# One block's decays and one of its key/query turns by DMA in place of TensorE, with the steps around them placed anew, in a fused linear-attention and bilinear-FFN kernel

## Chip, cores and metric

The kernel runs on 1 core of one Trainium2 chip. The metric is device microseconds from launch to end, less is better. Engines in the profile: PE is TensorE's matmul, PEld its weight load, DVE is VectorE, ACT is ScalarE, POOL is GpSimd, SP is SyncE, which here only issues DMAs.

## What is computed

The reference is a gated linear attention followed by a bilinear feed-forward layer:

```python
batch, n_heads, seq, head_dim = (4, 8, 768, 48)      # q, k, v, alpha
for t in range(S):
    state = alpha[:, :, t, :, None] * state + np.einsum('bhd,bhe->bhde', k[:, :, t], v[:, :, t])
    y[:, :, t] = np.einsum('bhd,bhde->bhe', q[:, :, t], state)
...
n_tokens, d_model, d_ff = (3072, 384, 1536)
x = np.ascontiguousarray(attn_out.transpose(0, 2, 1, 3)).reshape(B * S, H * D)
a = x @ w_a
b = x @ w_b
return (a * b @ w_out).astype(np.float32)
```

Inputs and output are float32; alpha lies between 0.8 and 1.0.

## The kernel before

The work is cut into six blocks, called chunks in the code and numbered 0 to 5. Block c holds the positions of third `c // 2` of the sequence (256 of 768) for two of the four batches; its two batches are its rows 0 and 1. Blocks 0 and 1 are the first third of the sequence, and the state goes from block 0 to 2 to 4 and from 1 to 3 to 5. Two neighbouring positions share a partition (`r`), and the 128 partitions are two halves (`g`) of 64, between which the state is carried on.

The whole order of work is written out by hand in the string `PROGRAM` (from L17). A line names a block and a list of steps; the table `OPS` maps each step's first word to a function, its arguments are a row, a half, a PSUM bank (0 to 7) or an engine (V = DVE, S = ACT, P = GpSimd, Y = SP). Each engine takes its own steps in the order in which they stand there, and waits where a step needs another engine's result, a bank that is still being read, or a buffer that is still in use. A step on one engine never overtakes an earlier one on the same engine. So the place of a step in `PROGRAM` matters only against other steps of its own engine or DMA queue.

The steps of a block, with those that the change and the prediction touch:

- `ld` loads q, k, v or alpha, from the queue of GpSimd or SP (L547). `Wo` loads the output weights. `ln`, `l2`, `l2s`, `ra` make logarithms of alpha, their pair sums `l2`, and `ra` (L554, L562, L611, L643).
- `H`, `L` split `l2` into a rounded part and a rest (L599, L605); `A2 u bank` sums them over the positions on PE (L636). In later blocks `R` and `AQ` do this (L621, L631).
- `E u b` and `E u i` take exponentials of that sum on ACT: `beta` and `invb` (L665). `lv` scales q by `ra` and k by alpha (L650). `mq`, `mk` write the scaled queries and keys into `QKp` (L676, on DVE).
- The decays of the state, one number for each batch, half, head and feature, go into the small tile `bl`. Two ways exist. `dk` makes them on PE with two-column matmuls (`decay_pe`, L698) and `de` takes the exponential on ACT (`decay_exp`, L719). Or `dr` stores the last row of each half of `beta` to a DRAM tile `row` (L682) and `dl` loads it back feature by feature into `bl` (L687); both are SP's DMAs, two for each step.
- Queries and keys have to be turned, features onto partitions. Two ways exist here too. `C u h bank` turns half a row's heads with eight PE transposes (`turn`, L736) and `Ce u h engine` copies the 1024 columns from PSUM into `kqT` (L958 on ACT or L960 on DVE). Or `T u` turns the whole row with one DMA transpose from SP (`turn_dma`, L745), and `Tr u engine` sorts the keys into another tile, `kp` (`turn_keys`).
- `K2` multiplies keys and values on PE (L805) into two banks, one for each half; `k u g` folds them into the state, using `bl` (`state`: L819, or L822 and L823; on DVE). The first half gives `Sm`, the second `S`.
- `D u h bank` makes scores on PE in two banks (L837), `Mc` with `Mm`, or `M`, masks them. `SB` and `SA` multiply the queries by the carried state and `Y` the scores by the values, both L866; `v`, `vs` prepare the values; `X` copies the result to `xT`.
- The feed-forward: `a f w bank` and `b f w bank` are three matmuls each (L921) for one of twelve groups f of 128 of the 1536 columns, 512 columns wide for both rows (`*`) or 256 for one row. `as` copies a's result from PSUM on ACT (L927), `pr` multiplies it by b's on DVE (L935), `o m half bank` is six matmuls for half the sum of output tile m (L943), `ot` copies it out and `st` stores it.

Until the change, blocks 0 and 1 use PE for decays and turns, and blocks 2 to 5 use DMA:

```python
def decay_rows(ch, us):
    for g in range(2):
        nc.sync.dma_start(out=ch.row[us, g:g + 1].rearrange("b g a r d -> g b (a r d)"),
                          in_=ch.beta[(g + 1) * HC - 1:(g + 1) * HC, us].rearrange("g b h d -> g b (h d)"))

def decay_load(ch, us):
    for r in range(2):
        nc.sync.dma_start(out=bls[ch.c % 2][r * DP:r * DP + D, us].rearrange("d b g a -> d (b g a)"),
                          in_=ch.row[us, :, :, r, :].rearrange("b g a d -> d (b g a)"), allow_slow_non_contiguous=True)

def turn_dma(ch, u):
    nc.sync.dma_start_transpose(out=alloc_t(ch, u).rearrange("p (x s) -> p x s", s=C), in_=QKp[ch.c % 2][:, u].rearrange("p j r h d -> p (j r h d)"))
```

Of the kernel before, what the change touches and what calls it, by code (L numbers as in the profile page):

```python
# [102 lines left out]
2: AQ 0; E 1 i; ld v * P; E 1 b  # L103
1: pr 2 0; a 10 0 4; as 10 0; a 7 0 5; M 1 0; a 1 0 6; Mm 1 1 V; b 4 0 7; pr 4 0; b 1 0 1; a 5 0 4; as 1 0
1: pr 1 0
2: lv 0 q P; E 0 b; dr
1: b 10 0 6; pr 10 0; a 6 0 7; as 7 0; b 7 0 1; pr 7 0; b 5 0 5; as 5 0
2: lv 1 k P
1: b 11 0 6; pr 5 0; SA 1
2: mq 0 V  # L110
1: Y 1
2: mq 1 V
1: b 6 0 1
2: mk 1 V; E 0 i
1: as 6 0; a 0 0 0; b 0 0 7; pr 6 0; a 11 0 4; X 1 S; a 2 1 5; b 3 0 2; as 0 0; pr 0 0; as 11 0; a 3 0 3
1: as 3 0; a 8 0 4; b 9 0 0; b 2 1 1; a 6 1 3; pr 11 0; as 2 1; a 9 0 5; as 9 0; pr 3 0; o 2 0 2
3: ln *; l2s 0 P; l2 0 P
0: st 0 Y
1: a 5 1 5; pr 2 1
# [1058 lines left out]
```

## Time and profile before

| | |
|---|---|
| median of 3 runs | 189.72 us |
| lowest and highest | 189.21 and 191.22 us |
| the profiled execution's own time | 190.44 us |
| its span, first to last instruction | 188.7 us |
| mean granted TensorE clock | 0.991 |
| DMA, whole execution | 29.43 MB, mean 156 GB/s |
| DMA queues of SP | 41.2% of 16 engines' span |
| DMA queue of GpSimd | 39.3% of 16 engines' span |

The profile shows one execution. Times in it count from the first instruction. In a group's row stand the line, the engine, the operation, the tiles (written <- read), the shapes and the count; then busy time, mean length, and the idle time before with what ended it. In a timeline a row has start, length, engine, line, operation and tiles, and in brackets the engine's idle time before it with its releaser. The chain of waits follows the work that ended last back to the start, so its shares add up to the span. Matmuls are pipelined: the step from one group's start to the next tells a group's price better than its length.

### The profile page before, as it was taken

The numbers are of one execution on the slowest core, as the hardware profiler recorded it, in microseconds if no ns is written. First come the engines' busy times: TensorE is split into PE (matmuls) and PEld (weight loads), VectorE is DVE, ScalarE is ACT, GpSimd is POOL, SyncE is SP. The second block draws the span as 40 slices with busy tenths as digits, with TensorE's granted clock in tenths as the row PEclk, the third lists the DMA queues.
The fourth block names the chain that finished last, engine by engine and source line by source line (L and its number), as shares of the span: only waits on it lengthen the run. The fifth ranks groups of instructions, "written<-read, shape, count | busy, mean of one in ns | idle before, by whom it ended". The sixth has DMA issues, their size and how long they took to land.

```text
span 188.7 us, 6347 instructions
## 1 busy us (share of the span) xinstructions
PE 181.9 (96%) x2693; PEld 122.3 (65%) x2709; DVE 152.6 (81%) x271; ACT 120.1 (64%) x228; POOL 53.6 (28%) x74
## 2 busy tenths in 40 slices
PE   7979999999999999999999999999999999999993
PEld 3969886566778886754445644555457477565992
DVE  2484889788979799998889899999999945696862
ACT  4364865579995797797697949965980451526230
POOL 8999654998062240003500003300000000000000
PEclk9987999999999999999999999999999999999999
DMA  5999999999999899989999699939500102110053
GB/s 125 263 225 195 261 235 254 230 231 257 247 214 129 129 215 276 275 237 182 198 173 271 144 116 167 112 107 165 89 0 9 43 0 83 44 43 0 0 170 127
DMA packets 66285, 29.43 MB, mean 156 GB/s; under 512 B 55776, under 2 KB 64624, under 8 KB 66256
## 3 DMA queue, kind: packets, MB, share of 16 engines
q1 hardware_dynamic: 47488, 16.34, 41.2%
q0 software_dynamic: 18624, 12.58, 39.3%
q8 instruction: 21, 0.34, 0.7%
q10 hardware_dynamic: 144, 0.10, 0.2%
q14 instruction: 8, 0.07, 0.1%
HBM read 25.98 MB, written 4.74 MB: 163 GB/s over the span
## 4 chain that ended last, share of the span: by engine, by line
PE 90%; ACT 6%; issue 2%; DVE 1%
PE psum L921 47%; PE psum L943 12%; PE psum L1032 11%; PE psum L866 5%; PE psum L837 3%; PE psum L589 2%; PE psum L590 2%; PE psum L736 2%; PE psum L572 2%; ACT vx L958 2%; PE psum L631 1%; ACT la L554 1%; PE psum L792 1%; PE psum L805 1%; PE psum L698 1%
## 5 line engine op out<-in xcount | busy, mean ns | idle before, releaser
L921 PE MATMUL psum<-xT,wb_t 128*128 128x512 bf16 (+1 forms) x263 | 55.8, 336 | 0.5 <-issue 0.2
L921 PE MATMUL psum<-xT,wa_t 128*128 128x512 bf16 (+1 forms) x262 | 55.2, 335 | 0.5 <-issue 0.2
L921 PEld LDWEIGHTS <-wa_t 128*128 128x128 bf16 x270 | 25.7, 98 | 19.2 <-issue 0.5
L921 PEld LDWEIGHTS <-wb_t 128*128 128x128 bf16 x270 | 25.5, 98 | 18.4 <-issue 0.5
L943 PE MATMUL psum<-wo_t,prod 128*128 128x384 bf16 x144 | 26.1, 327 | 0.0
L958 ACT ACTIVATE ot<-psum 128x384 f32<-128x384 f32 (+1 forms) x23 | 11.2, 487 | 17.7 <-PE psum L1032 15.4
L650 POOL TENSOR_TENSOR q_t<-q_t,ra 128x384 f32<-128x384 f32 x6 | 6.4, 1072 | 53.6 <-ACT ra L643 31.1
L943 PEld LDWEIGHTS <-prod 128*128 128x128 bf16 x144 | 13.3, 98 | 8.3
L958 ACT ACTIVATE vx<-v_t 32x384 bf16<-32x384 bf16 x26 | 13.5, 521 | 1.5 <-DVE vx L771 1.1
L1032 PEld LDWEIGHTS <-prod 128*128 128x128 bf16 x144 | 12.0, 98 | 1.2
L850 ACT ACTIVATE m<-psum 128x768 bf16<-128x768 f32 x14 | 11.0, 810 | 2.3 <-PE psum L837 2.3
L676 DVE TENSOR_TENSOR QKp<-q_t,beta 128x768 bf16<-128x768 f32 x10 | 9.4, 952 | 1.9 <-ACT beta L665 1.6
L554 ACT ACTIVATE la<-a_t 128x1536 f32<-128x1536 f32 (+2 forms) x9 | 9.5, 1054 | 1.7 <-DMA a_t<-in_alpha_dram 1.5
L676 DVE TENSOR_TENSOR QKp<-k_t,invb 128x768 bf16<-128x768 f32 x10 | 10.1, 1013 | 0.3
L846 DVE TENSOR_TENSOR m<-psum,mask 128x768 bf16<-128x768 f32 x10 | 9.5, 949 | 0.6 <-PE psum L837 0.6
L1044 DVE TENSOR_TENSOR ot<-psum,ot 128x384 f32<-128x384 f32 x9 | 5.0, 555 | 5.9 <-issue 3.2
L866 PE MATMUL psum<-m,vx 64*64 64x128 bf16 (+1 forms) x576 | 8.7, 205 | 0.0
L547 POOL DMA_DIRECT2D v_t<-in_v_dram x8 | 8.5, 1064 | 0.0
L866 PE MATMUL psum<-kqT,Sm 64*64 64x128 bf16 x144 | 7.5, 220 | 0.4 <-DVE Sm L819 0.4
L866 PEld LDWEIGHTS <-vx 64*64 64x64 bf16 x576 | 7.6, 108 | 0.1
L854 DVE TENSOR_TENSOR m<-m,mask 128x768 bf16<-128x768 bf16 x14 | 7.4, 550 | 0.0
L665 ACT ACTIVATE prod<-psum 128x384 f32<-128x384 f32 x8 | 3.5, 488 | 6.0 <-PE psum L590 6.0
(292 smaller groups left out, 361.5 us busy)
## 6 DMA issues: line engine op xcount, KB each, us to landing
out_dram<-ot SPq DMA_DIRECT2D x23, 192.0 KB, 2.7
q_t<-in_q_dram SPq DMA_DIRECT2D x3, 768.0 KB
k_t<-in_k_dram SPq DMA_DIRECT2D x3, 768.0 KB
a_t<-in_alpha_dram POOLq DMA_DIRECT2D x2, 768.0 KB, 11.7
v_t<-in_v_dram POOLq DMA_DIRECT2D x4, 384.0 KB, 7.6
a_t<-in_alpha_dram SPq DMA_DIRECT2D x2, 768.0 KB
a_t<-in_alpha_dram POOLq DMA_DIRECT2D x3, 384.0 KB, 7.5
k_t<-in_k_dram POOLq DMA_DIRECT2D x3, 384.0 KB, 7.3
```

What stands on the lines that cost most here:

```text
L547: eng.dma_start(out=t[:, us, hs].rearrange("p b h r d -> p (b h) (r d)"), in_=src[ch.b0 + us.start:ch.b0 + us.stop, hs, ch.s * 2 * C:(ch.s ...
L554: nc.scalar.activation(out=ch.la[:, us, hs].rearrange("p b h r d -> p (b h r d)"), in_=ch.a[:, us, hs].rearrange("p b h r d -> p (b h r d) ...
L650: eng.tensor_mul(x, x, by)
L676: eng.tensor_mul(QKp[ch.c % 2][:, u, j, :, hs, :D], src[:, u, hs].rearrange("p h r d -> p r h d"), f)
L846: nc.vector.tensor_mul(m, x, maskn())
L850: nc.scalar.activation(out=m, in_=x, func=AF.Copy)
L854: eng.tensor_mul(m, m, maskn())
L866: nc.tensor.matmul(o, lhsT=lhsT, rhs=rhs, start=(g, c) not in begun, stop=False, skip_group_check=True)
L921: nc.tensor.matmul(p, lhsT=(wa_t, wb_t)[w][:, kk, f * 128:(f + 1) * 128], rhs=ch.xT[:, kk, us, :], start=(kk == 0), stop=(kk == KT - 1))
L943: nc.tensor.matmul(op, lhsT=ch.prod[:, f, at:at + C], rhs=wo_t[:, f, :], start=(f == 0), stop=(f == NFF - 1))
L958: nc.scalar.activation(out=o_, in_=i_, func=AF.Copy)
L1032: nc.tensor.matmul(o[:, g], lhsT=A[:, f, g * C:(g + 1) * C], rhs=W[:, f], start=(not more and (apart or g == 0) and f == 0), stop=(f == LH ...
```

## The change

Only `PROGRAM` differs, by one line more, so every line number behind it is one higher. Block 1's `dk *` and `de *` go, and `dr 0`, `dl 0`, `dr 1`, `dl 1` come: its decays go through DRAM, each row by itself, nine new DMA issues on SP with the transpose. For row 1 of block 1, `C 1 0`, `C 1 1` and their two copies `Ce` go, and `T 1` with `Tr 1 S` comes; row 0 keeps its PE transposes. All other steps stay, with other places and other PSUM banks in the stretch between; GpSimd's queue keeps its order. The diff, cut:

```diff
--- before.py
+++ after.py
@@ -40,114 +40,115 @@
 0: pr 1 1
-1: ra 0; lv 0 q P; ld k 1 P
-0: a 5 1 3; pr 5 0; as 3 1; b 0 1 1; Wo 6 12; as 4 1; b 2 1 4; pr 3 1; a 10 * 5
-1: H 1 V; L 1 V
-0: a 11 * 7; as 0 1; as 2 1; pr 2 1
-1: ra 1
-0: b 5 1 0; b 10 * 2
+1: ra 0
+0: as 4 1
+1: H 0 V; ra 1
+0: pr 5 0; as 0 1
+1: L 0 V
+0: b 0 1 3
+1: lv 0 q P
+0: a 5 1 7
+1: ld k 1 P
+0: Wo 6 12; a 10 * 4; b 2 1 2; as 3 1; pr 0 1; pr 4 1
+1: H 1 V; A2 0 1
+0: a 6 * 3; pr 3 1; b 10 * 5
+1: E 0 b; L 1 V
+0: as 10 *; pr 10 *; as 5 1; a 8 * 6
+1: E 0 i; dr 0
+0: b 5 1 4; pr 5 1; as 2 1; b 9 * 7; b 11 * 5; a 9 * 4; as 9 *; b 6 * 0; pr 2 1; a 11 * 1; as 11 *; as 6 *
+1: A2 1 2; E 1 b; mq 0 V
+0: b 8 * 4; pr 9 *; a 7 * 1; b 7 * 3
+1: lv 0 k V
 2: ld a * P
-0: pr 4 1; as 10 *
 1: ld v 1 P
-0: pr 0 1; b 6 * 1
 2: ld q * P
-0: as 5 1
-1: H 0 V; L 0 V; lv 1 q P; A2 0 3; lv 1 k P
-0: a 8 * 6; pr 5 1; pr 10 *
-1: E 0 b
-0: a 7 * 0; b 7 * 2
-1: mq 0 V
-0: b 11 * 4
+1: lv 1 q P; lv 1 k P; mk 0 V; dl 0
+0: pr 11 *; pr 6 *; as 7 *
+1: C 0 1 7
 2: ld k * P
-1: lv 0 k V; E 0 i; mk 0 V
-0: as 11 *; pr 11 *; a 6 * 3; as 7 *
-1: A2 1 0
 3: ld v * P
-1: E 1 b
-0: cz 1 v P; c3 P; pr 7 *
+1: C 0 0 5
+0: as 8 *; pr 8 *
+1: Ce 0 1 V; K2 0 0 6 0; v 0 S
+0: o 3 0 1
 1: E 1 i
-0: as 6 *; pr 6 *
-1: dk * 7; de *
-0: a 9 * 5; as 9 *; b 8 * 0
-1: C 0 1 7; mq 1 V; Ce 0 1 V; C 0 0 2
-0: b 9 * 1; pr 9 *; o 2 0 3; as 8 *; pr 8 *
-1: Ce 0 0 S; D 0 0 4; Mc 0 0; K2 0 0 2 6
-0: o 0 0 7; o 3 0 0
-1: k 0 0 V; k 0 1 V; SB 0 4
+0: o 2 0 2; pr 7 *
+1: vs 0 1 S
+0: o 1 0 7
+1: k 0 0 V; Ce 0 0 S; SB 0 3; mq 1 V; mk 1 V; k 0 1 V; D 0 0 5; vs 0 0 S; Mc 0 0; Mm 0 0 V
+0: o 3 1 -; o 1 1 -
+1: D 0 1 5; dr 1; T 1
+0: o 2 1 -; ot 1 S
+1: dl 1
+0: ot 3 V
+1: SA 0
+2: ln *
+0: cz 1 v P
+1: M 0 1
+0: ot 2 S
+1: Y 0
+0: o 0 0 0; o 0 1 -
+1: v 1 V; vs 1 1 V; X 0 S; a 2 0 1; a 4 0 3; b 4 0 2; K2 1 1 4 5; vs 1 0 S
+0: c3 P
+2: l2s 0 V; l2 0 V; l2s 1 V; R 0
+0: ot 0 S
+2: R 1
+1: k 1 0 V; b 2 0 0; as 2 0; pr 2 0
 3: ld a * P
-1: mk 1 V; D 0 1 1; M 0 1
-0: o 3 1 -; ot 3 V; st 3 Y
-1: v 0 S; vs 0 0 S; vs 0 1 S; Mm 0 0 V; C 1 1 6; Ce 1 1 V
-2: ln *
-0: o 0 1 -; ot 0 S
-1: C 1 0 2; Ce 1 0 S; v 1 V; vs 1 0 S
-0: o 1 0 0; o 1 1 -; ot 1 S
-1: SA 0; Y 0
-2: l2s 0 V
-1: K2 1 1 2 1; X 0 S
 0: cs 1 0 P
-2: l2 0 V
-1: D 1 1 6; Mc 1 1
-0: o 2 1 -; ot 2 S
-1: a 2 0 0; as 2 0; a 4 0 4
-2: l2s 1 V
-1: b 2 0 5
-2: ra 1; lv 1 q P
-1: vs 1 1 V
-2: R 0
-1: D 1 0 6; as 4 0; k 1 0 V
+1: as 4 0; pr 4 0; Tr 1 S; a 10 0 1; as 10 0; k 1 1 V; D 1 1 6
+2: AQ 3
+1: Mc 1 1; D 1 0 0; M 1 0; SB 1 1
+2: ra 1
+1: a 7 0 5
+2: E 0 i
+0: st 3 Y
...
 2: ra 0
-1: SB 1 2
-2: R 1
-1: k 1 1 V
-2: AQ 0; E 1 i; ld v * P; E 1 b
-1: pr 2 0; a 10 0 4; as 10 0; a 7 0 5; M 1 0; a 1 0 6; Mm 1 1 V; b 4 0 7; pr 4 0; b 1 0 1; a 5 0 4; as 1 0
...
+2: dr
...
-2: T 1
-2: dl
...
-2: Tr 1 S; K2 * * 4 5; k * 0 V
+2: T 1; dl; T 0
+3: ln *
+1: b 3 1 3; pr 3 1; o 2 0 1
+2: v 1 S
+1: b 9 0 5; a 9 1 6; b 9 1 3; as 5 1; pr 5 1; b 6 1 4; as 9 0; pr 9 0; as 9 1
+2: K2 * * 7 0
...
+2: Tr 1 S
+1: as 4 1; b 11 1 3; as 11 1; pr 6 1; a 1 1 4; b 7 1 2; as 10 1
+2: k * 0 V; v 0 S; k * 1 V
+1: b 4 1 5; pr 4 1; as 1 1; b 10 1 0; pr 11 1; o 2 1 -
...
-2: v 0 S; T 0
...
-2: D 0 0 0
...
+2: Tr 0 V; D 0 0 5; vs 1 0 V
```

More of the change, by code (lines that the diff above doesn't have):

```diff
@@ new lines @@
+0: cs 1 0 P
+1: as 4 0; pr 4 0; Tr 1 S; a 10 0 1; as 10 0; k 1 1 V; D 1 1 6
[5 more added lines that the diff above has]
+0: st 3 Y
+2: lv 1 q P
+1: b 10 0 6
+2: E 0 b
+1: pr 10 0; Mm 1 1 V; b 1 0 7; as 7 0; b 7 0 0
+2: E 1 b
+1: b 5 0 3; a 1 0 6
+2: mq 1 V
+1: as 1 0; pr 1 0; a 5 0 5; as 5 0
+2: lv 0 k V
+1: SA 1; Y 1
+2: E 1 i; ld v * P
+1: b 8 0 5; a 11 0 4; pr 7 0
+2: ra 0
+1: a 8 0 6; b 11 0 7; b 6 0 0; pr 5 0; X 1 S; b 2 1 1; as 8 0; as 11 0; b 0 0 6; a 0 0 2; pr 11 0; pr 8 0
@@ new lines @@
+1: a 6 0 7; b 3 0 3; a 3 0 4
+2: lv 0 q P; lv 1 k P; mk 1 V
+1: as 6 0; pr 6 0; as 0 0; a 3 1 5; b 5 1 7; a 2 1 2; as 3 0; a 8 1 0; pr 3 0; pr 0 0; as 2 1; a 5 1 4
+2: mk 0 V
+1: as 8 1; b 8 1 6; pr 2 1
+2: mq 0 V
+1: as 3 1; a 6 1 2; pr 8 1; a 9 0 0
+2: dr
+0: st 0 Y
+2: T 1; dl; T 0
[4 more added lines that the diff above has]
+2: K2 * * 7 0
+4: ld a * Y
+1: a 10 1 6; as 6 1; a 4 1 2; pr 9 1; a 11 1 5
+2: Tr 1 S
@@ L151 @@
+1: as 4 1; b 11 1 3; as 11 1; pr 6 1; a 1 1 4; b 7 1 2; as 10 1
+2: k * 0 V; v 0 S; k * 1 V
+1: b 4 1 5; pr 4 1; as 1 1; b 10 1 0; pr 11 1; o 2 1 -
+3: ld q * Y
+1: a 0 1 3
+3: ra 1
+1: a 7 1 4; ot 2 S; as 0 1
+3: ra 0
+1: pr 10 1
+2: Tr 0 V; D 0 0 5; vs 1 0 V
+3: l2s 0 P; l2 0 P; l2s 1 P; R 0
+1: as 7 1
+2: D 1 1 0; M 1 1
+1: b 1 1 3; pr 1 1; o 0 0 7
 2: vs 0 0 V
```

37 lines of the change are left out of this document (removed).

## The prediction

> **What bounds the kernel now.** I read the page's busy times first, then the chain of waits, then the windows around the change, then the timelines of single engines and the landing times of the DMAs. From the page:
>
> ```profile
> PE 181.9 (96%) x2693; PEld 122.3 (65%) x2709; DVE 152.6 (81%) x271; ACT 120.1 (64%) x228; POOL 53.6 (28%) x74
> DMA  5999999999999899989999699939500102110053
> PE 90%; ACT 6%; issue 2%; DVE 1%
> ```
>
> TensorE (PE) is busy 181.9 of 188.7 us and is 90% of the chain that ended last. The DMA digits are 9 nearly throughout until about slice 28 (132 us). The windows of the stretch in question (the columns are length, busy time of PE, PEld, DVE, ACT, POOL, granted clock, DMA share, GB/s):
>
> ```profile
> 41.00:46.00 5.00, 5.00 (x98) 3.10 (x96) 4.20 (x8) 3.98 (x8) 5.00 (x6) 1.00 1.28 267
> 46.00:51.00 5.00, 5.00 (x137) 3.58 (x135) 4.87 (x10) 4.75 (x7) 0.38 (x1) 1.00 1.18 254
> 61.00:66.00 5.00, 5.00 (x45) 4.19 (x44) 3.89 (x9) 3.58 (x8) 1.37 (x2) 1.00 0.81 120
> ```
>
> PE is busy 5.00 of 5.00 us at full clock in each. So work taken off PE here shortens the kernel by its own length, and no placement can find idle PE time to fill; a wait that PE gets costs its own length. The DMA share is 1.18 to 1.28 where block 1's new transfers would run, and 0.81 where block 2 does such transfers today.
>
> **What is taken off PE.** The chain of waits has the decays and block 1's transposes (start, length, what); the other rows are used below as prices of PE steps:
>
> ```profile
> 33.47 3.25 PE psum L921 x15
> 37.08 0.82 PE psum L698 x32
> 37.90 0.16 issue
> 39.30 0.89 PE psum L736 x16
> 41.82 0.30 PE psum L837 x16
> 42.11 0.25 PE psum L805 x32
> 44.42 0.17 PE psum L866 x2
> 47.83 1.95 PE psum L943 x12
> 57.78 0.81 PE psum L866 x41
> 58.59 4.04 PE psum L921 x36
> ```
>
> The 32 matmuls of `dk` cost 0.82 us and a switch of 0.16. Row 1's `C 1 0; C 1 1` are 16 transposes like the 16 of row 0 in the row of 39.30: 0.89. Together 1.87 us, all in the chain: that is the most the change can win, 1.0% of 189.72. Off the path go two exponentials and a copy of 1024 columns on ACT, for which one copy of the same size (`Tr 1 S`) comes, and one such copy on DVE.
>
> **What the rearrangement costs by itself.** Matmul groups keep their shapes; only banks and order differ. Two new bank waits are seen in the order. `a 5 1` now takes bank 7, read by `pr 5 0`, and that product stands behind the cast `H 0` on DVE; `b 10 1` takes bank 0 right behind block 2's `K2`, whose reader `k * 1` stands behind `k * 0`. Each is due within a product's step of its reader, so each costs between 0 and one DVE step (0.63 by the pair of product rows below); I take 0.15 each, 0.3 in all. The GpSimd queue keeps its order, loads included, so no load is issued behind a different step; what a slower load would hold up is taken in with the rivals.
>
> **The decays through DRAM.** Rows from the timelines of PE, ACT, DVE and SP, and the landing line of the block 2 transfer into `bl`:
>
> ```profile
> 32.77 0.53 PE L636 MATMUL psum<-lh,utr 128*128 128x384 f32 x1
> 33.51 0.49 ACT L665 ACTIVATE beta<-psum 128x384 f32<-128x384 f32 x1 [1.75 <-PE psum L636]
> 38.74 0.60 ACT L927 ACTIVATE as__779<-psum 128x512 bf16<-128x512 f32 x1
> 39.23 0.59 ACT L927 ACTIVATE as__813<-psum 128x512 bf16<-128x512 f32 x1
> 37.11 0.73 DVE L935 TENSOR_TENSOR prod<-as__738,psum 128x512 bf16<-128x512 bf16 x1
> 37.74 0.71 DVE L935 TENSOR_TENSOR prod<-as__744,psum 128x512 bf16<-128x512 bf16 x1
> 46.94 0.68 DVE L960 COPY kqT<-psum 128x1024 bf16<-128x1024 bf16 x1
> 42.52 0.36 DVE L819 TENSOR_TENSOR Sm<-psum,bl 128x192 bf16<-128x192 f32 x1 [0.23 <-PE psum L805]
> 57.91 1.81 DVE L676 TENSOR_TENSOR QKp<-q_t,beta 128x768 bf16<-128x768 f32 x2
> 56.04 1.32 SPq L682 DMA_DIRECT2D row<-beta x2
> 62.45 1.78 SPq L687 DMA_DIRECT2D bl<-row x2
> DMA to landing us min/median/max: 2.5/2.5/2.5
> ```
>
> Take the start of `A2 0` as zero. `beta` is ready at 1.23 (33.51 + 0.49 - 32.77). `dr 0` issues until 2.55, its second transfer from about 2.0. The trace has no landing for `row`; the nearest row is the 2.5 us of `bl`, the same kind of transfer, in the quiet stretch, and the loaded end is 4.4 (2.5 times the factor 1.75 found below). So `row` is there at 4.5 to 6.4; `dl 0` issues for 1.78, its second transfer about 1.2 in, and lands 2.5 to 4.4 later: at 8.2 to 12.0. The first reader, `k 0 0` on DVE, is due after this PE work: two `A2` of 0.53, eleven groups of 512 columns at 0.65 (3.25 for 15 matmuls, three to a group) and `b 5 1` at 0.34 (4.04 for twelve groups of 256): 8.55 to the start of `C 0 1`. Then comes `pr 8` at +0.7 (`a 7`, two groups before `C 0 1`, then two ACT copies 0.49 apart), and pr 8, `Ce 0 1`, `pr 7` at 0.63, 0.68 and 0.63: 2.64. So `k 0 0` is due at 11.2, and `bl` comes between 3.0 early and 0.8 late. I take no wait. Behind `k 0 0` on DVE stand `mq 1`, `mk 1` and the next products, so lateness here would move all of block 1.
>
> **The DMA transpose.** `T 1` needs `mq 1` and `mk 1`, and both stand behind `k 0 0`: from the start of `C 0 1`, 2.64 + 0.40 (the 0.36 of Sm and a handover) + 0.90 + 0.95 = 4.9 us. The reader on PE is `D 1 1`, with `Tr 1` on ACT (1.05, below) in between. PE work from `C 0 1` to `D 1 1` in the new order: two `C` 0.89, two `K2` 0.50, eight half output groups at 0.975 to 1.03 (1.95 for two; I take 1.0) 8.0, `SB` 0.17, two `D` 0.60, `SA` with `Y` 0.81, five groups of 256 at 0.337, 1.7: 12.7 us. So the transpose may take 12.7 - 4.9 - 1.05 - 0.1 = 6.65 us from issue to landing before PE waits. What it takes, and two GpSimd loads of the same 384 KB into `v_t`, each row followed by its landing line:
>
> ```profile
> 66.43 1.05 ACT L958 ACTIVATE kp<-kqT 128x1024 bf16<-128x1024 bf16 x1
> 60.67 1.59 SPq L745 DMA_TRANSPOSE kqT<-QKp  x1
> DMA to landing us min/median/max: 4.4/5.4/6.4
> 54.38 1.19 POOL L547 DMA_DIRECT2D v_t<-in_v_dram  x1
> DMA to landing us min/median/max: 5.5/5.5/5.5
> 91.14 1.21 POOL L547 DMA_DIRECT2D v_t<-in_v_dram  x1
> DMA to landing us min/median/max: 9.6/9.6/9.6
> 92.08 0.74 SPq L547 DMA_DIRECT2D a_t<-in_alpha_dram  x1
> 40.89 1.20 POOL L547 DMA_DIRECT2D k_t<-in_k_dram  x1
> 44.70 1.17 POOL L547 DMA_DIRECT2D a_t<-in_alpha_dram  x1
> ```
>
> The eight transposes of today land in 4.4 to 6.4 us, and all run when GpSimd's queue has little or nothing under way. The same load of `v_t` lands in 5.5 us alone and in 9.6 with SP's loads issued a microsecond behind it: sharing with another queue costs a factor of 1.75. Block 1's `T 1` is issued near 44 us, between GpSimd's 768 KB loads of 40.89 and 44.70, where the window moves 254 to 267 GB/s. So bounds are 4.4 (no sharing) and 11.2 (6.4 x 1.75); I take 5.4 x 1.75 = 9.4, because a transfer against a full GpSimd queue is nearer to the 9.6 row than to the 5.5 row. That is 2.8 us later than the 6.65 allowed, and PE waits that long at `D 1 1`; ACT waits in `Tr 1`, with `as 10 0` and `Mc 1 1` queued behind. [...]
>
> `dl 1` is issued behind `T 1` on SP and its data follow in the same queue, so `k 1 0` on DVE, with `pr 2 0` and `pr 4 0` behind it, gets its decays at about the transpose's landing; this wait lies beside PE's and I add nothing for it, at most 1.0 for a landing behind the transpose's.
>
> **The sum.** Against the profiled execution: -1.87 + 0.3 + 2.8 = +1.2 us on 190.44, its own time (span 188.7 and 1.74 around it). Those 190.44 are 0.72 above the median of the runs, 189.72; on the median the forecast is 189.72 + 1.2 = 190.9 us.
>
> **The rivals.**
> The transpose lands in time: it takes no more than 6.65 us, as all eight of today's do. For it: every recorded landing. Against it: none of these ran against a full GpSimd queue. Then -1.87 + 0.3 = -1.6: 188.1 us, and 187.8 if even the bank waits cost nothing. Chance 0.25.
> The decays of row 0 are late: `k 0 0` holds DVE. The `bl` transfers are 384 separate 4-byte values for each r, the finest in the kernel, and may suffer from a full queue by more than the factor 1.75 of long rows. It decides from a landing about 1 us behind the 11.2 due, since `SB 0` on PE then waits as well, and every microsecond more goes on top of the late transpose, because `T 1` starts behind it. With 2 to 4 us of it: 190.9 + 2 to 4, 193 to 195 us, slower. For it: the upper bound of 12.0 is past the due time already; against: the middle is 1.1 early. Chance 0.18.
> The transpose is a little late, under 1.5 us: between 188.1 and 189.6. Chance 0.10.
> That the transposing and the decays stay on PE is excluded: the order of instructions has neither `dk` nor row 1's `C`.
>
> **How the numbers follow.** The forecast, a transpose late by 1.5 to 4.6 us (11.2 - 6.65), has 0.47 and gives 189.6 to 192.8; 190.9 is its middle by the rows. A measurement of this kernel tells about 1% (1.9 us) from no change: the three runs span 189.21 to 191.22. Faster than 187.8 needs the whole 1.87 with no wait at all: 0.07, out of the first rival. Slower than 191.6 needs a transpose late by about 3.5 us (0.20 of the forecast's 0.47) or the late decays (0.18): 0.38. Within 1%: the rest, 0.55. The range, 188.0 to 194.0, leaves out the tail above 194 and the few cases below 188.
>
> **What would show it.** `L698` is gone and `L736` has 48 transposes; the landing of the first transpose is 9 us or more; PE's first `L837` of row 1 shows some 3 us idle, put down to ACT `kp`; DVE's `L819` of row 1 waits for the DMA of `bl` in the same stretch. Wrong would be: landings of 5 to 6 us and no PE gap (first rival), or a PE gap at the row 0 output groups with `L819` of row 0 waiting for `bl` (second rival), or a loss behind the replaced stretch, where the order of steps is the old one again.

## The result: 10% slower, and where the profile shows it

The changed kernel takes 209.12 us in the median of 5 runs (207.70 to 210.58), the kernel before 189.72 beside it (188.84 to 191.22): a ratio of 1.102, 95% interval 1.093 to 1.111. The forecast was 190.9 with a range to 194.0. Medians and ratios leave out one run in a slower state (195.72 us, of the kernel below that has the transpose in the old order). The profiled execution after is one of 209.12 us with a span of 207.3. Its page, the lines of busy time, granted TensorE clock, DMA share and GB/s in 40 slices of 5.2 us, and the chain by engine:

```profile
PE 185.1 (89%) x2646; PEld 121.9 (59%) x2661; DVE 152.0 (73%) x270; ACT 120.1 (58%) x226; POOL 52.2 (25%) x74
...
PEclk9999999985995599999999999999999999999999
DMA  6999999999999096999599995982960010211034
GB/s 162 248 208 238 219 258 246 259 244 234 102 88 84 3 114 106 196 278 277 165 190 208 241 246 112 176 75 82 134 115 3 3 38 5 76 38 41 0 129 140
...
PE 59%; DMA 27%; ACT 7%; issue 3%; DVE 2%; SPq 1%; POOL 1%; POOLq 0%; DVEq 0%
```

DMA is now 27% of the chain, where it had none. Compare the DMA and GB/s rows in slices 10 to 12 (52 to 67 us): the DMA engines are 90% busy or more and move 84 to 102 GB/s, where slices 1 to 9 move 208 to 259 at the same share. Busy engines that move little are the mark of this result. The chain of waits names two transfers (start, length, what):

```profile
31.33 4.01 DMA row<-beta
35.42 0.32 SPq L688
...
35.79 9.12 DMA bl<-row
...
45.03 0.06 DVE Sm L820
...
47.16 20.33 DMA kqT<-QKp
67.50 1.06 ACT kp L959
...
68.61 0.57 PE psum L838 x10
```

The decays of row 0 land 9.12 us after their issue, the transpose 20.33 us. What PE and DVE lost to them is in the view of waits (total, times, longest):

```profile
ACT kp L959 <- DMA kqT<-QKp: 12.1, 2, 11.3
...
PE psum L838 <- ACT kp L959: 11.6, 2, 11.4
```

PE stood 11.4 us at row 1's scores, and 2.9 us at row 0's output groups (its row stands below). GpSimd's loads beside the transpose suffered as well; the issue rows of block 3's `v` and alpha, each followed by its landing line, after and then before:

```profile
40.87 1.17 POOL L548 DMA_DIRECT2D v_t<-in_v_dram  x1
DMA to landing us min/median/max: 23.0/23.0/23.0
42.93 1.17 POOL L548 DMA_DIRECT2D a_t<-in_alpha_dram  x1
DMA to landing us min/median/max: 23.7/23.7/23.7
```

```profile
42.07 1.17 POOL L547 DMA_DIRECT2D v_t<-in_v_dram  x1
DMA to landing us min/median/max: 12.6/12.6/12.6
```

Alpha, issued at 44.70 in the kernel before, also landed after 12.6 us there. Both needed some 11 us more than before, so neither of these loads gained what the transpose lost. The windows of after show the consequences for PE (length, busy PE, PEld, DVE, ACT, POOL, clock, DMA share, GB/s), and its timeline the first gap:

```profile
41.00:46.00 5.00, 2.12 (x30) 1.28 (x30) 0.96 (x2) 2.04 (x3) 3.60 (x5) 0.87 1.34 240
46.00:51.00 5.00, 5.00 (x40) 2.30 (x35) 3.01 (x7) 1.52 (x3) 0.00 (x0) 0.50 1.31 234
...
57.00:63.00 6.00, 0.21 (x2) 0.00 (x0) 0.00 (x0) 0.00 (x0) 0.00 (x0) 0.90 1.33 85
```

```profile
45.45 0.32 PE L867 MATMUL psum<-kqT,Sm 64*64 64x128 bf16 x2 [2.88 <-DVE Sm L820]
```

Behind the first gap PE ran five microseconds at a granted clock of 0.50. From 57 to 63 us no compute engine did more than 0.3 us of work, and the DMA still moved only 85 GB/s. Comparing the start of the same steps on ACT in both profiles, the changed kernel is 1.2 us ahead where the kernel before is at 24 us, 17.0 us behind at 77 us and 18.7 behind at the end: nearly all of the loss lies in the replaced stretch.

### The profile page after: what moved, and what is told of

Read it like the earlier page. It is cut to its first block, busy times and chain, and to the rows that moved or that the text cites. A ratio compares the mean times of both kernels' runs of the same rounds, so it can differ in the third digit from the quotient of the medians.

```text
span 207.3 us, 6253 instructions
## 1 busy us (share of the span) xinstructions
PE 185.1 (89%) x2646; PEld 121.9 (59%) x2661; DVE 152.0 (73%) x270; ACT 120.1 (58%) x226; POOL 52.2 (25%) x74
## 4 chain that ended last, share of the span: by engine, by line
PE 59%; DMA 27%; ACT 7%; issue 3%; DVE 2%; SPq 1%; POOL 1%; POOLq 0%; DVEq 0%
PE psum L922 33%; DMA kqT<-QKp 12%; PE psum L1033 10%; DMA q_t<-in_q_dram 5%; PE psum L944 5%; DMA bl<-row 4%; PE psum L867 4%; DMA v_t<-in_v_dram 3%; PE psum L838 2%; DMA row<-beta 2%; ACT vx L959 2%; ACT la L555 1%; PE psum L632 1%; ACT kp L959 1%; DVE QKp L677 1%
## 5 line engine op out<-in xcount | busy, mean ns | idle before, releaser
L944 PE MATMUL psum<-wo_t,prod 128*128 128x384 bf16 x144 | 28.1, 347 | 0.0
L651 POOL TENSOR_TENSOR q_t<-q_t,ra 128x384 f32<-128x384 f32 x6 | 6.9, 1152 | 75.3 <-DVE tmp L823 25.9
L959 ACT ACTIVATE ot<-psum 128x384 f32<-128x384 f32 (+1 forms) x23 | 11.2, 485 | 20.9 <-PE psum L1033 16.0
L944 PEld LDWEIGHTS <-prod 128*128 128x128 bf16 x144 | 14.1, 103 | 9.8 <-issue 2.2
L838 PE MATMUL psum<-kqT,kp 64*64 64x128 bf16 (+1 forms) x288 | 6.3, 214 | 11.6 <-ACT kp L959 11.6
L820 DVE TENSOR_TENSOR Sm<-psum,bl 128x192 bf16<-128x192 f32 x4 | 1.4, 355 | 17.4 <-PE psum L838 12.9
L959 ACT ACTIVATE kp<-kqT 128x1024 bf16<-128x1024 bf16 x6 | 6.3, 1054 | 12.2 <-DMA kqT<-QKp 12.1
L838 PEld LDWEIGHTS <-kp 64*64 64x64 bf16 x288 | 4.8, 113 | 14.2 <-ACT kp L959 12.0
L1033 PEld LDWEIGHTS <-prod 128*128 128x128 bf16 x144 | 12.0, 98 | 1.2
L867 PE MATMUL psum<-kqT,Sm 64*64 64x128 bf16 x144 | 8.1, 227 | 3.2 <-DVE Sm L820 3.2
L677 DVE TENSOR_TENSOR QKp<-k_t,invb 128x768 bf16<-128x768 f32 x10 | 9.5, 955 | 0.2
```

Source lines behind the costliest of these rows:

```text
L651: eng.tensor_mul(x, x, by)
L677: eng.tensor_mul(QKp[ch.c % 2][:, u, j, :, hs, :D], src[:, u, hs].rearrange("p h r d -> p r h d"), f)
L838: nc.tensor.matmul(s2[g * HC:(g + 1) * HC, r, p, cols(x)], lhsT=keysT(ch, u, 2 * h + p, g, rs, x), rhs=queriesT(ch, u, 2 * h + p, g, rs, x ...
L867: nc.tensor.matmul(o, lhsT=lhsT, rhs=rhs, start=(g, c) not in begun, stop=False, skip_group_check=True)
L944: nc.tensor.matmul(op, lhsT=ch.prod[:, f, at:at + C], rhs=wo_t[:, f, :], start=(f == 0), stop=(f == NFF - 1))
L959: nc.scalar.activation(out=o_, in_=i_, func=AF.Copy)
```

## The experiments

The theories at the outset. A: the transpose beside GpSimd's loads is the main loss. B: the new order of steps is. C: the 4-byte decay loads are, and the transpose suffers only with them. Unless said otherwise a kernel is the changed one with the edit shown, and its time is of one run; of long lines a diff shows only the steps around the change. The kernel before ran beside each at 188.7 to 191.3 us.

**The change taken apart: one part at a time.** First the transposing back on TensorE:

```diff
-1: D 0 1 5; dr 1; T 1
+1: D 0 1 5; dr 1
-1: Y 0
+1: Y 0; C 1 1 7; C 1 0 5; Ce 1 1 V
-X 0 S; a 2 0 1
+X 0 S; Ce 1 0 S; a 2 0 1
-pr 4 0; Tr 1 S; a 10 0 1
+pr 4 0; a 10 0 1
```

> The changed kernel with row 1 of block 1 turned by PE transposes again (C and Ce in place of T and Tr); its decays still go through DRAM. Theory A, the DMA transpose in the loaded stretch is the main loss: the 11.6 us gap of PE before row 1's scores and the slow clock behind it (about 2 us) go, and the gap of 3.0 us at SB of row 0 with its slow clock (about 3 us) stays, since bl of row 0 still lands some 9 us after its issue; 0.9 us of transposes come back, DVE gets one more copy (about 1 us of waits). About 195 us, 193 to 198. Theory B, the new order of steps is itself the loss: above 203. Theory C, the 4-byte decay loads are the main loss and the transpose only waits with them: above 203 as well, with bl of row 1 landing late and holding k 1 0.

195.07 us, as A had it: with no transpose, 14 us of the loss are gone. The decays alone still cost PE a gap; who waited for `bl`, and its landings in this kernel:

```profile
  PE psum L867: 3.1, 1
...
DMA to landing us min/median/max: 8.6/9.0/9.5
```

So this load of 1.5 KB takes some 9 us in this stretch, beside GpSimd's loads, with or without a transpose. Next the opposite half, decays on TensorE, the transpose kept:

```diff
-1: E 0 i; dr 0
+1: E 0 i
-0: b 8 * 4; pr 9 *; a 7 * 1; b 7 * 3
+0: b 8 * 4; pr 9 *
+1: dk * 7; de *
+0: a 7 * 1; b 7 * 3
-mk 0 V; dl 0
+mk 0 V
-1: D 0 1 5; dr 1; T 1
+1: D 0 1 5; T 1
-1: dl 1
```

> The changed kernel with block 1's decays from PE again (dk and de, no dr or dl for block 1); the DMA transpose T 1 stays. Theory A: the transpose still lands 15 to 20 us after its issue, PE still waits about 11 us before row 1's scores; the gap at SB of row 0 goes. About 203 us, 200 to 206. Theory C: without the 4-byte values the transpose lands within 8 us and the time is near 190 us. Theory B: above 203 with the loss spread over many small waits.

208.32 us. C falls: without a single decay load the transpose takes as long. Its issue on SP and its landing line:

```profile
45.54 6.15 SPq L747 DMA_TRANSPOSE kqT<-QKp  x1
```

```profile
DMA to landing us min/median/max: 21.4/21.4/21.4
```

The number was missed by 5 us: the transpose starts earlier here and waits longer. Then both parts back on TensorE (both edits together), which leaves the order of steps:

> Both undone in the new order: decays and row 1's turn on PE, only the order and the banks of the change are left. Theories A and C: 191 to 192.5 us, because DVE gets back a copy of 0.7 us in a stretch that has little room (about 1.9 us of small waits counted through the order); landings of all loads as in the kernel before. Theory B: 203 or more.

193.73 us in the median of 4 runs, ratio 1.025 (1.018 to 1.032). B falls as the main cause, but A's figure is missed: this kernel loses 3.4 to 6.1 us to the one before. A second profile of the same kernel:

> The change's order alone (decays and row 1's turn on TensorE) once more, for a second profile of it: its four times were 191.8 to 194.5 us and the one profiled was the fastest, in which the named gaps of TensorE come to only some 2 us more than in the kernel before. Expected: 192 to 195 us. If the order's cost is in waits of TensorE, its idle time in this profile is larger than in the first by as much as the time is; if it is not, the matmuls themselves take longer (the granted clock or the steps between them).

195.94 us. PE's gaps sum to 1.5 us more than in the first profile, by a wait at 111 us behind a late load of alpha, which landed at 108.4; a granted clock of 0.8 from 10 to 19 us accounts for some 2 more (0.2 of 9 us, an estimate) of the 4.1 between the two times. Both have in common that 2.8 us are lost to the kernel before between the same two instructions of PE, at 25 and at 72 us. Where, the window of 50 to 58 us shows, before and then with the order alone:

```profile
50.00:58.00 8.00, 8.00 (x202) 6.35 (x196) 6.62 (x15) 7.17 (x17) 4.12 (x4) 1.00 1.25 204
```

```profile
50.00:58.00 8.00, 6.81 (x123) 5.09 (x122) 7.82 (x15) 5.30 (x13) 2.14 (x2) 1.00 0.79 156
```

```profile
PE psum L633 <- DVE Sm L821: 0.7, 1, 0.7
...
PE psum L923 <- DVE m L848: 0.5, 1, 0.5
```

DVE is busy 7.82 of 8.00 us there and by the view of waits PE waits 1.2 us for it: in this kernel DVE is the bound of this stretch. But the kernel has the copy `Ce 1 1 V` (0.69 us on DVE, at 48.64), which the changed kernel leaves out. In the next two kernels, where the transpose lands in some 5 us and that copy is absent, DVE is busy 7.33 and 6.07 us of these 8; how much of the loss the order causes in the changed kernel itself isn't shown.

**The loads taken from beside the transpose.** All three of GpSimd's loads are held until the transpose has landed (`gatet 1` copies one element of its result on GpSimd, so its queue waits):

```diff
-2: ld k * P
-3: ld v * P
-3: ld a * P
 0: cs 1 0 P
+1: gatet 1
+2: ld k * P
+3: ld v * P; ld a * P
```

> The changed kernel, but GpSimd issues the loads of k of block 2 and of v and alpha of block 3 only after T 1 has landed (GpSimd reads one value of its result first). Theory A, the transpose is slow because GpSimd's loads run beside it: T 1 lands within 5 to 8 us; the gap before row 1's scores falls from 11.6 to under 2 us; the gap at SB of row 0 stays or shrinks (fewer loads beside bl). 191 to 196 us, unless the later loads are missed further on. If the transpose is slow for another reason of its own (its place, the small bl transfers in SP's queue), it still lands at 15 us or more and the time stays above 203.

198.16 us. The transpose on SP, and GpSimd's copy that waited for it:

```profile
47.75 1.42 SPq L746 DMA_TRANSPOSE kqT<-QKp  x1
```

```profile
53.03 0.38 POOL L1065 CAST go<-kqT 1x1 f32<-1x1 bf16 x1 [11.76 <-DMA kqT<-QKp]
```

5.3 us in place of 20.3, with the same order, the same place and row 1's decay loads behind it. A's central claim holds; the time came out 2 us over its range, since the held loads are late further on. With alpha alone issued beside the transpose, by a copy on GpSimd (`gateq`) that waits for row 1's scaled keys (the diff is against the kernel with all three held):

```diff
-1: D 0 1 5; dr 1; T 1
+1: D 0 1 5; dr 1; T 1; gateq 1
+3: ld a * P
-3: ld v * P; ld a * P
+3: ld v * P
```

> The changed kernel with the GpSimd loads held until the transpose has landed, as in the run with every load held, except one: block 3's alpha (768 KB, not converted), which is issued when row 1's keys are scaled, so that it runs beside the transpose alone with the decays' loads of row 1. Theory A: one load beside it is enough, the transpose lands 10 us or more after its issue (5.6 us with every load held), and a gap of several us opens ahead of row 1's scores, 200 to 206 us. If it takes several loads in the queue, or the converting loads of v, the transpose lands within 8 us and the time stays at 197 to 200 us.

195.32 us; issue at 47.59, GpSimd's copy at 52.49, 4.9 us. A's forecast for it didn't come, but the run doesn't test it: alpha, issued at 48.14, has its first packet at 51.72, when 2039 of the transpose's 2048 packets had begun. So the two were hardly under way together. The same pairing with the decays on TensorE (both edits together) has the transpose issued 3 us earlier:

> The change's order with the decays back on TensorE, so that only the transpose of row 1 is left of it, and with the loads out of the transpose's way: block 3's alpha is issued just behind the transpose (that pairing did no harm), block 2's keys and block 3's v once it has landed. If order, decays and collision add up, the decays' gap of 3 to 3.7 us at row 0 is gone, the transpose lands within 6 us, and the time is that of the change's order alone, 192 to 194.5 us. If a quiet transpose still costs time of its own (late loads, a row that waits for the copy behind it), 195 to 198 us. If the transpose pays what it takes off TensorE, below 192 us.

203.10 us, over every range that was expected. The transpose on SP, the copy of keys on ACT that waited for it, and a window in between:

```profile
44.47 5.11 SPq L748 DMA_TRANSPOSE kqT<-QKp  x1
```

```profile
62.45 1.06 ACT L961 ACTIVATE kp<-kqT 128x1024 bf16<-128x1024 bf16 x1 [10.58 <-DMA kqT<-QKp]
```

```profile
54.00:56.00 2.00, 0.00 (x0) 0.00 (x0) 0.09 (x1) 0.00 (x0) 0.00 (x0) 1.00 1.26 62
```

18 us: block 2's q was still moving when it was issued, and alpha joined in. In this window no compute engine does more than 0.1 us of work, and the DMAs move 62 GB/s, so it is not the compute engines that slow the transfers there.

**In the kernel before.** The loads of `v` put beside block 2's transpose:

```diff
-3: ld v * P
 1: E 1 b
...
-2: AQ 0; E 1 i; ld v * P; E 1 b
+2: AQ 0; E 1 i; E 1 b
...
 2: lv 1 k P
+2: ld v * P
+3: ld v * P
```

> The kernel before, with only this changed: block 2's and block 3's loads of v on the GpSimd queue are issued right behind block 2's last pre-scaling there (about 57.6 us) instead of earlier, so that they run beside block 2's DMA transpose of row 1, which is issued at about 60.7 us and landed within 4.4 to 6.4 us in the kernel before, where the GpSimd queue was quiet then. Theory A (a transposing DMA and loads of the GpSimd queue hold each other up far beyond a fair share): that transpose lands 10 us or more after its issue, the v loads need over 12 us, TensorE waits for row 1 of block 2, and the time is 194 to 204 us. Rival (they share the engines fairly, a factor of about 1.75): the transpose lands within 8 to 11 us, and the time is 190 to 193 us. If the collision needs the 4-byte decay loads as well, those of block 2 are issued only behind the transpose, and the transpose lands in under 8 us.

191.36 us in 9 runs, ratio 1.011 (1.008 to 1.015): not A's. The transpose was issued at 60.29 and its reader started at 67.30: 7.0 us, under the rival's range for it, within the rival's for the time, and as the third reading had it, which the run with decays on TensorE had excluded. It says little on A, though, for the two hardly met: the transpose's first packet began at 63.70 us, and only 402 of its 2048 before the last of `v` at 64.52. And the transpose for row 1 in the old order, loads held, decays on TensorE:

```diff
-2: ld k * P
...
-3: ld v * P
...
-3: ld a * P
-1: mk 1 V; D 0 1 1; M 0 1
+1: mk 1 V; T 1; D 0 1 1; M 0 1
-1: v 0 S; vs 0 0 S; vs 0 1 S; Mm 0 0 V; C 1 1 6; Ce 1 1 V
+1: v 0 S; vs 0 0 S; vs 0 1 S; Mm 0 0 V
-1: C 1 0 2; Ce 1 0 S; v 1 V; vs 1 0 S
+1: v 1 V; vs 1 0 S
 0: cs 1 0 P
+1: gatet 1
+2: ld k * P
+3: ld a * P; ld v * P
-1: D 1 1 6; Mc 1 1
-1: a 2 0 0; as 2 0; a 4 0 4
+1: a 2 0 0; as 2 0; a 4 0 4; Tr 1 S
-1: b 2 0 5
+1: b 2 0 5; D 1 1 6; Mc 1 1
```

> The kernel before, in its own order and with its decays on TensorE, where only row 1 of block 1 is turned by a DMA transpose: it is issued behind the scaling of row 1's keys and ahead of block 0's store on the SP queue, the GpSimd loads that would run beside it (keys of block 2, alpha and v of block 3) are held until it has landed, and row 1's scores go behind two steps of the experts. Theory A: with the loads away the transpose lands in 5 to 7 us and no gap opens at row 1's scores; TensorE saves the 0.9 us of row 1's turn, and the loads, some 10 us later, cost between nothing and 4 us further on (they cost about 2 us in the kernel with every load held): 188.5 to 193 us, most likely 190. If the change's order of steps was what kept the time up in the kernel with every load held, 188 to 189.5 us. If a transpose in block 1 costs time by itself, the transpose needs over 9 us and the time is above 194 us.

194.15 us in the median of 5 runs, ratio 1.023 (1.017 to 1.028). 8.3 us to the landing, while q was still moving; PE waits 2.3 us for ACT's copy behind it and 0.9 for the mask that ACT applies next. No version with the transpose in block 1 was as fast as the kernel before.

**Which load.** Alpha alone held, then `v` alone in the same way, then alpha held in the kernel with decays on TensorE:

```diff
-3: ld a * P
 0: cs 1 0 P
+1: gatet 1
+3: ld a * P
```

> The changed kernel, where only block 3's alpha load (packets of 4224 bytes) is held until row 1's transpose has landed; the loads of block 2's keys and of block 3's v stay as they are, ahead of the transpose in the GpSimd queue and still moving when it is issued. Dose (transpose and loads crawl as long as packets of both are in flight, whichever loads they are): less is left to move than in the changed kernel, the transpose lands 11 to 16 us after its issue instead of 20.3 us, and the time is 201 to 206 us. Large packets are what crawls (the other kernel's loads of v, packets of 192 bytes, met a transpose without harm): only v is left from about 52 us on, the transpose lands within 10 us, 196 to 200 us. Small packets are what crawls: 18 to 21 us, 206 to 210 us.

198.49 us; 48.63 to 57.60, 9.0 us.

> The other half of the same test: only block 3's load of v (packets of 192 bytes) is held until row 1's transpose has landed; block 2's keys and block 3's alpha (packets of 4224 bytes) stay ahead of the transpose. Dose: 11 to 16 us from issue to landing, 201 to 206 us. Large packets are what crawls: 14 to 20 us, 203 to 209 us. Small packets are what crawls: the transpose lands within 10 us, 196 to 200 us.

197.54 us; 48.07 to 58.07, 10.0 us. By the words of the two expectations the first is a hit for large packets and the second for small ones, so neither stands on these times; taking either load away halves the landing, more than the dose allowed. With `v` held, the transpose got its first packets only at 52 us, when alpha was nearly through. The packets speak for the large ones: with alpha held, beside `v` alone, 377 to 416 transposing packets begin in each microsecond from 53 to 55; with `v` held there are 77 and 181 at 54 and 55 us, beside the last of alpha, and 1010 at 56, behind it.

> The changed kernel with its decays on TensorE (208.32 us, transpose 21.4 us from issue to landing, gap of 14 us ahead of row 1's scores), and here one edit more: block 3's alpha load is held until the transpose has landed. Large packets crawl: beside v's small packets alone the transpose lands 8 to 12 us after its issue (the end of q's and the keys' loads still lies in front of it), the gap ahead of row 1's scores shrinks to 1 to 5 us, and the time is 195 to 200 us. If it is the number of loads and not their packets: 12 to 17 us and 200 to 205 us. If alpha has nothing to do with it: 18 us or more, 206 us or more.

199.20 us against 208.32, 13.7 us against 21.4, PE's wait 6.5 against 14.2. The time is the large-packet theory's, the landing that of the number of loads. The packet records of the trace tell more than the times. Packets that began in a microsecond, by size, with their mean length in ns (256 bytes: the transpose; 192: `v`; 4224: alpha, q, keys), in the kernel with decays on TensorE and alpha not held:

```
us     4224 B      192 B      256 B
53     none        368 x 35   368 x 31
54     4 x 296     350 x 35   354 x 31
56     8 x 872     48 x 149   54 x 206
57     11 x 1142   61 x 111   117 x 112
```

Beside `v` alone the two queues get on packet for packet, 368 and 368, `v`'s at 35 ns (35 to 36 in the changed kernel before its transpose moves), the transpose's at 31 (in block 2 of the kernel before, with none of GpSimd's loads beside it, four in five take 18 to 22 ns). When alpha's large packets arrive both collapse, to 54 and 48 in the microsecond from 56 on. What a collapse consists of, in the kernel with alpha beside the transpose and decays on TensorE (start in us, what, lengths in ns):

```
51.456-51.497  256 B x14: 22, 236 to 252 (x9), 448 to 461 (x4)
51.516         4224 B: 220
51.696-51.732  256 B x17: 20, 222 to 232 (x14), 448, 451
51.747         4224 B: 227
51.927-51.963  256 B x22: 22, 235 to 246 (x16), 448 to 452 (x5)
51.982         4224 B: 220
```

In this half microsecond one large packet begins as the other ends, and 14, 17 and 22 transposing packets begin within some 40 ns, ahead of each large one. In each of these batches every transposing packet but one takes one or two of the large one's lengths, and the one that takes 20 to 22 ends just where the large one begins. The changed kernel has the same steps: from 63.30 to 63.83 us three batches of 14 to 17 begin 0.23 to 0.24 us apart, with lengths of 20 to 22, 221 to 248 and 448 to 466 ns, beside one large packet of 222 to 225 at a time. I read it so, and it is an inference: transposing packets advance together, and all of a batch wait for the large one. How a packet of one load can hold them no run shows. It covers only part of the collapse: beside the packets shown, another large one lasts 2304 ns (50.778 to 53.082), and from 54 us on 9 to 14 large packets are under way at once in this kernel, many of them for over 1000 ns.

Alpha cut into two transfers, row by row, was to send it in packets of 192 bytes (in the changed kernel, then with decays on TensorE):

```diff
+        if what == "a" and ch.c == 3:
+            for r in range(2):
+                eng.dma_start(out=t[:, us, hs, r].rearrange("p b h d -> p (b h) d"),
+                              in_=src[...].rearrange("b h (p r) d -> r p (b h) d", r=2)[r])
+            return
```

> The changed kernel, in which only block 3's alpha load is cut into two transfers, one for each of the two rows that lie side by side, so that the same bytes go at the same place of the queue in packets of 192 bytes instead of 4224. In the slow stretch of the changed kernel one 4224-byte packet of 220 to 230 ns runs at a time while the transpose's packets on the other engines, 18 to 22 ns alone, take 222 to 252 or 448 to 467 ns, one or two of its times: the transposing packets seem to advance together, held by the engine that moves a large one. Theory (the large packet is what holds them): beside 192-byte packets the transpose's packets take 31 to 36 ns and get every second turn, the transpose lands 9 to 14 us after its issue instead of 20.3, and the time is 197 to 202 us. Rival (it is the bytes or the number of loads that wait): 18 us or more, 206 us or more, as in the changed kernel or worse, since 4096 small packets take longer than alpha's 190 large ones.

> The same cut of alpha's load into 192-byte packets in the changed kernel with its decays on TensorE (208.32 us with alpha in large packets, transpose 21.4 us; 199.2 us and 13.7 us with alpha held). Theory: the transpose lands 12 to 16 us after its issue, as with alpha held or a little later, and the time is 198 to 202 us. Rival: 20 us or more and 207 us or more.

209.30 and 201.81 us, landings of 17.9 and 16.6. The cut didn't do what it was for: the trace still has packets of 4224 bytes, 1408 in place of 1424. These two say nothing on the size. Alpha on SP's queue instead, behind the transpose and the decays:

```diff
 1: dl 1
+3: ld a * Y
...
-3: ld a * P
```

> The changed kernel, where only block 3's alpha load goes to SP's queue, right behind the transpose and the decay loads of row 1, instead of GpSimd's: it is still asked for at once, and no large load of another queue is left beside the transpose but the end of block 2's keys. Theory (what crawls is the transpose among packets of large loads from the other queue): as with alpha held, the transpose lands 8 to 11 us after its issue, no gap of over 1.5 us is left ahead of row 1's scores, the gap of 3 to 4 us at row 0 stays, and the time is 195 to 199 us. If alpha's traffic as such does it, whatever its queue: 14 us or more from issue to landing, 203 us or more.

198.46 us; issue 47.09, reader at 56.55, 9.4 us, and PE waits 1.8 in place of 11.4. Behind the transpose in its own queue alpha does little harm. It goes in packets of 384 bytes there, the first at 55.65 us, and the last packet of 4224 bytes (50.21) is over before the transpose's first (50.96); so no large packet was beside the transpose, and the run doesn't tell the queue from the packet size.

**PE kept busy in the gaps**; the multiplies of `fill` are read by nobody:

```diff
-1: k 0 0 V; Ce 0 0 S; SB 0 3; mq 1 V
+1: k 0 0 V; Ce 0 0 S; fill 14 4; SB 0 3; mq 1 V
-k 1 1 V; D 1 1 6
+k 1 1 V; fill 50 6; D 1 1 6
```

> The changed kernel with TensorE given useless multiplies into a bank to do in its two long gaps: 14 ahead of row 0's product with the scores (SB 0) and 50 ahead of row 1's scores (D 1 1). They change no wait on a DMA. In the changed kernel's profile the granted TensorE clock stood at 0.5 for some 5 us behind the two gaps, and the matmuls there took about 320 ns instead of 163. If that clock comes of TensorE having idled, it stays near 1.0 here, the landings stay (9 us for the decays, about 20 us for the transpose) and the time falls by the 3 to 5 us that the slow clock cost: 204 to 206.5 us. If the slow clock has another cause (the DMA traffic, the chip's load), or costs nothing in the end because the path waits for the loads anyway, the time stays at 208 to 210 us.

208.34 us in 4 runs, ratio to the kernel before 1.100 (1.094 to 1.106). Clock, and the reader of the transpose:

```profile
PEclk9999999999999799999999999999999999999999
```

```profile
67.22 1.06 ACT L959 ACTIVATE kp<-kqT 128x1024 bf16<-128x1024 bf16 x1 [13.96 <-DMA kqT<-QKp]
```

The 0.5 of the clock came of PE's idling: with the multiplies the mean granted clock is 0.992, in the changed kernel 0.959. But it cost nothing: near 55 us this kernel is 2.9 us ahead of the changed one, and then it waits for the same landing. The length of a gap alone doesn't tell whether a slow clock follows: one followed a gap of 2.9 us in the changed kernel (0.50 from 46 to 51 us) and one of 3.25 us in this one (the 7 in the row of the clock), and none followed one of 3.1 in the first experiment (mean clock 1.000).

**By themselves.** Behind the last store of the kernel before, transfers one after the other, GpSimd copying an element of each result as it lands:

```diff
+BENCH = "T; a; v; dl; a T; v T; a v T; T a; a dl; T dl; qY; qY T; a T; T"
...
+5: bench
```

> The kernel before, with a row of transfers added behind its last store, when nothing else runs, each step begun when the one before it has landed: a transpose alone; block 5's alpha load alone (768 KB, GpSimd); its v load alone (384 KB as stored, GpSimd, converting); the two decay loads alone; alpha and then the transpose, which starts while alpha is moving; v and then the transpose; alpha, v and then the transpose; the transpose and right behind it alpha; alpha and then the decay loads; the transpose and the decay loads behind it; a plain load of q on SP's own queue; that load and the transpose behind it; alpha and then the transpose again; the transpose alone again. If the collision is between a transposing DMA and any load of GpSimd that moves beside it: alone the transpose takes 4 to 6 us and alpha 5 to 7 us, together both take 12 us or more, far over the sum. If two transfers merely share: together they end within the sum of the two, 9 to 13 us. If large packets alone do it, v and the transpose end within their sum and alpha and the transpose do not. If it needs the rest of the kernel (TensorE, the other engines' traffic into the same memory) the pairs all end within their sums here.

GpSimd's timeline: alpha is issued, a copy into `QKp` lets the transpose go, and `go` copies mark the landings.

```profile
184.34 0.18 POOL L1078 CAST QKp<-go 1x1 bf16<-1x1 f32 x1
189.20 0.17 POOL L1075 CAST go<-kqT 1x1 f32<-1x1 bf16 x1 [4.69 <-DMA kqT<-QKp]
189.83 1.16 POOL L550 DMA_DIRECT2D a_t<-in_alpha_dram  x1 [0.46 <-issue]
196.16 0.17 POOL L1075 COPY go<-a_t 1x1 f32<-1x1 f32 x1 [5.17 <-DMA a_t<-in_alpha_dram]
...
205.56 1.16 POOL L550 DMA_DIRECT2D a_t<-in_alpha_dram  x1 [0.41 <-issue]
206.71 0.18 POOL L1078 CAST QKp<-go 1x1 bf16<-1x1 f32 x1
212.35 0.17 POOL L1075 COPY go<-a_t 1x1 f32<-1x1 f32 x1 [5.47 <-DMA a_t<-in_alpha_dram]
214.09 0.17 POOL L1075 CAST go<-kqT 1x1 f32<-1x1 bf16 x1 [1.56 <-DMA kqT<-QKp]
```

Alone the transpose takes 4.9 us (184.34 to 189.20), alpha 6.3; together 8.5, with 7.4 for the transpose. Every other pairing ends within its sum too, from the transpose with the decay loads (5.2 us, alone 4.9 and 2.3) to `v` and the transpose (9.0, alone 5.6 and 4.9) and alpha, `v` and the transpose (11.3, alone 16.8 in sum). Alpha asked for 0.4 us behind the transpose delays it as well, to 8.0 us (235.78 to 243.80). The two decay loads take 2.3 us alone and at most 6.1 behind alpha. The same with large loads waiting behind `v`'s (`BENCH = "T; v a T; v a; v a T; a v T; v q a T; v q a; a q T; v a dl; v a"`):

> Again a row of transfers behind the last store of the kernel before, now in orders in which the transpose begins while a large load still waits behind v's: v, alpha and then the transpose (twice); v and alpha alone; alpha, v, transpose; v, q, alpha and then the transpose; v, q, alpha alone; alpha, q, transpose; v, alpha and the decay loads; v and alpha alone again. In the last run alpha and v were first and the transpose got its turn as they ended; all pairs ended within their sums (alpha and transpose 8.5 us, alone 6.2 and 4.5). Theory now: what crawls is the transpose's packets among packets of 4224 bytes (alpha, q, keys), not among v's of 192. Then v, alpha, transpose and v, q, alpha, transpose end more than 4.5 us, the transpose's own time, behind the same loads without it, by 8 us or more, and alpha, v, transpose ends within 12 us as before. Rival: in the quiet nothing crawls, whatever the order; every row ends within the loads' own time plus 4.5 us. Then the collapse needs something of the kernel that is absent here, and its inner cause stays open.

The rival: `v`, q, alpha and the transpose end 13.4 us after the first issue (235.20 to 248.55), the loads alone 11.8 (249.11 to 260.87). The transpose itself takes 9.9 us (238.64 to 248.55), twice its 4.9 alone. In its packets, at 243 to 245 us, the transpose gets 37 and 58 packets in a microsecond beside 57 and 55 of 4224 bytes at 262 and 263 ns (their median at 48 us in the kernel before, with no transpose under way, is 265), and 1012 when the loads have ended. So while both move, from 243.1 to 245.8 us, it waits, packet for packet, but holds up nothing. Why the same mixture crawls inside the kernel stays open.

## Why the prediction was wrong, step by step

- **PE is the bound, and 1.87 us come off it.** The instructions went, but what was won can't be told from the runs. The kernel with decays in DRAM and PE's turn took 195.07 us in its one run, the one with both on PE 191.81 to 195.94 in five. The kernel whose transpose lands in 4.9 us took 195.32, no less than that with PE's turn; but its granted clock was 0.80 from 37 to 50 us and 0.90 from 50 to 58, where the other's was 1.00.
- **The rearrangement, 0.3 us.** The term failed in size: 3.4 to 6.1 us, with PE's turn of row 1 and its copy on DVE included. I had looked for new bank waits of PE. What the profile of that kernel shows is DVE at 7.82 of 8.00 us, a bound that a count of banks doesn't see. 2.8 us are accounted for in the stretch; the rest of the median is open.
- **Decays: due 11.2, landing 8.2 to 12.0, "I take no wait".** From the start of `A2 0` (29.84) `row` came at 5.5 (forecast 4.5 to 6.4) and DVE was free for its reader at 10.9: both right. The landing of `bl` failed: 9.12 us from issue, where 2.5 x 1.75 = 4.4 was the upper end. It came at 15.1, DVE waited 4.3 us and PE 2.9. The second rival had this mechanism and this mark in the profile, at 0.18; I bounded a transfer of 4-byte pieces by the factor of long rows, though the rival says why it may not hold.
- **The transpose: 4.4 to 11.2 us, taken as 9.4, a wait of 2.8.** Place, reader and waiting engines were right (PE at row 1's scores behind ACT's copy); the size was off: 20.33 us and 11.4. The step that failed is the sharing factor 1.75 taken as an upper end. It is right for pairs in the quiet (7.4 against 4.9), too low for three loads ahead in the quiet (9.9), and false in block 1, where 23 us for both loads show a loss of throughput, not a share of it. The factor came of two plain loads, of 192-byte and 384-byte packets: beside packets of 4224 bytes the quiet transpose, with 256, got 58 packets in a microsecond, and 1012 when the loads had ended. The trace of before also had a row from the stretch itself, which the forecast didn't use: `v`, issued at 42.07, lands after 12.6 us, 2.3 times the 5.5 (partly a wait for the loads ahead in its own queue: its first packet began at 49.12). Without loads (5.3) or with alpha behind it on its own queue (9.4) the same transpose would have met the forecast or beaten it.
- **First rival (in time, 188.1).** False in block 1 as it was; and where the transpose did land in some 5 us the kernels still took 195.32 and 198.16 us.
- **The account.** By medians and single runs: order with PE's turn 4.8 (193.73 against 188.96 beside it), decays 1.3 (195.07 - 193.73), transpose among loads 14.0 (209.12 - 195.07). These add up to the whole because each is one kernel's time less the next one's, so the sum proves nothing. Undone the other way round, the transpose is worth 14.6 (208.32 - 193.73) and the decays 0.8 (209.12 - 208.32). 195.07 and 208.32 are single runs, and both figures for the decays lie within the spread of one kernel's runs; the transpose's 14 stand either way.

## What to carry to other kernels

Before a transfer is moved to the DMA queues, look at what the other queue has under way when it is issued, and for a transposing one let that queue run dry of large loads, or put them behind it on its own queue: here the landing then took 5.3 and 9.4 us in place of 20.3. A price from a quiet stretch times a sharing factor is no upper bound for such a transfer: here it gave at most 11.2 us, and the landing took 20.3. A new order is to be checked for every engine's load in each stretch, not only for the waits of the one that bounds the whole.

## What the hardware showed that I had not expected

- In block 1 a transposing DMA and GpSimd's loads, among them alpha's in packets of 4224 bytes, crawled side by side: 84 to 102 GB/s at a DMA share of 90% and more for some 15 us, in the last 10 of which (57 to 67 us) PE worked 0.21 us and no other compute engine at all. In block 2 of the kernel before four in five transposing packets took 18 to 22 ns; here a quarter of them took 218 ns or more.
- 1.5 KB in 4-byte pieces took 8.6 to 9.5 us in block 1, beside GpSimd's loads, where the same load in block 2 takes 2.5.
- While the transfers crawled, SP itself was held issuing the next ones: its two `bl` loads took 10.7 us to issue, so the store behind them was late as well.
